# The down projection's weight is read once, in rows of 1 KB, and held in two slots to the middle of the kernel

## Chip, cores and metric

The kernel runs on one core of one Trainium2 chip. The metric is device microseconds for one execution. Before the change the median of three runs is 1683.2 us (1682.9 to 1683.74).

## The reference, cut to what matters

One decode step of a transformer block (4 batch rows, model width D = 512, 32 heads of width 128, a cache of 4096 keys per head, a gated feed-forward of width F = 1792) and its gradients:

```python
q = (layernorm(x) @ wq)                      # 4 x 32 heads
p = softmax(q . k_cache * Dh**-0.5)          # over 4096 keys
h = x + (p . v_cache) @ wo
hh = silu(layernorm(h) @ w1) * (layernorm(h) @ w3)
h2 = h + hh @ w2                             # first output
# then the vector-Jacobian product with grad_out: gradients of x, k_cache, v_cache, wq, wo, w1, w3, w2
```

The caches hold 128 (batch, head) pairs of 1 MB each for K and for V. K is read once and V twice, and two gradients of the size of the caches are written, so nearly all of the 707 MB that the kernel moves are cache. The weight w2 of the change is 1792 x 512 in bf16, 1.8 MB. Two things need it: the gradient of hh, which is grad_out @ w2 transposed, and the block's own output h2.

## The kernel before, in words

**Slots.** One arena in SBUF is cut into 23 slots (`NSLOT`), each large enough for one head of K or V (1 MB over 128 partitions). The list `free` holds the free ones, the one freed longest ago first. `Slot(name)` takes one (L120 on), `give` puts it back. All of this is decided when the program is built, and so are the order of the instructions on each engine and the waits; a DMA into a slot waits until whatever used the slot last has ended. All loads of caches and weights and all large stores are issued by SyncE (SP), in the order in which the code makes them.

**Forward, 64 groups of two heads** (the loop over `gi`). In group gi, with a = 2 gi, the engines do this in the order of the code:

- PE makes the scores of heads a and a+1 from their transposed keys (`S_head`, L392) and gives back the two slots of transposed keys.
- PE and VectorE (DVE) transpose the keys of the next two heads, na = a+2 and nb = a+3, into new slots: `T_pe` (PE, L360, copied out by ScalarE, ACT, L361) and `T_dve` (DVE, L366). A head's keys must have landed for that.
- The softmax of the group goes over DVE, PE and ACT in turn: row maximum (L399, L404, L409, L416), exponential (L424), sum and reciprocal (L430, L435).
- `PK_mul` (DVE, L459) multiplies keys by probabilities, first for head a-1, later in the group for head a; after it the head's K slot is given back and `more_K` loads further heads (L181) while fewer than 8 are held and **more than one slot is free**.
- `M_mm` (PE, L474) multiplies V with that product for heads a-3 and a-2; `M_end` (L484, L488) copies the result into one of eight slots that collect such results (a new one every 16 heads, `Ms`), and gives back the slots of V and of the product; `load_V` (L189) then loads a further V. Three V are held.

The two K loads of a group are thus issued one after `M_end` of head a-3 and `PK_mul` of head a-1, the other after `M_end` of head a-2. The more slots are held by other things, the fewer heads of K are under way.

**w2, first reading.** From group 2 on a generator of side units, `d_hh_units`, is stepped once a group. It loads w2 into two slots (`load_w2`, L543, a row p of the tile holds the 14 weight rows 14 p to 14 p + 13, 7 KB in a row for each slot), transposes it (PE L565, ACT copy L566 into two more slots, where the columns are spread with a stride of 14), gives the two slots of w2 back after some ten groups, and multiplies with grad_out into `d_hhT`.

**End of the forward pass and middle.** From group 61 on free slots go to the last V heads, then to wo (four pages, L591, in rows of 1 KB), w1 and w3 (L585, rows of 3.5 KB). After the last group `attn_page` (PE L522) makes attention times wo in four pages, the layer norm of h follows, and the gate and up projections (PE L918). At the start of this middle part V is loaded for the second time into every slot that is free (`load_V2`, L871: seven heads here, two more after w1 and w3 are done). `w13T` (PE L606, copies by ACT L255 and DVE L257) transposes w1 and w3 in place, in units of up to eight blocks; DVE computes the activations, the last of them `hhT_bf` (L944). Then PE forms `dn_ps` (L952), the gradient that goes back through w1 and w3; from it come the gradient of h, the replicated rows and the first stores of V's gradient (`grad_V`, DVE L844, store L855).

**Backward.** From there on the kernel streams: V's second half in pairs of heads (L1335), the two gradients made by DVE (L844, L1438) and stored (L855, L1310, L1448). A second generator, `side_work`, makes the small outputs in between, stepped twice a head from head 35 on: the gradient of x and wq, then **w2, second reading** (L1143), the transposed rows of hh, a second transposition of hh in the order of w2's rows (L1166 on), the output matmuls (L1174), the DVE add with h (L1180) and the store of the first output (L1182, issued by GpSimd, POOL); then the gradients of w2, w1, w3 and wo.

Of the kernel before, what the change touches and what calls it, by code (L numbers as in the profile page):

```python
# [9 lines left out]
FP32 = mybir.dt.float32  # L10
BF16 = mybir.dt.bfloat16
ALU = mybir.AluOpType
# [16 lines left out]
def kernel(  # L29
# [22 lines left out]
    nc = tc.nc  # L52
    P = nc.NUM_PARTITIONS

    B = A_x.shape[0]
    D = A_x.shape[-1]
# [10 lines left out]
    FC = F // P  # L67
# [7 lines left out]
    x2 = A_x.rearrange("b s d -> (b s) d")  # L75
    g2 = grad_out.rearrange("b s d -> (b s) d")
    o0_2 = out_0.rearrange("b s d -> (b s) d")
# [24 lines left out]
    pers = ctx.enter_context(tc.tile_pool(name="pers", bufs=1))  # L102
# [7 lines left out]
    free = deque(range(NSLOT))  # L110
# [51 lines left out]
            gave(self.i, self.i + 1)  # L162


    rows_t = pers.tile([32 + B, D], FP32, name="rows_t")
    xr, xhat = rows_t[0:B, :], rows_t[32:32 + B, :]
    nc.gpsimd.dma_start(out=xr, in_=x2)
    gr_s = Slot("gr")
# [33 lines left out]
    ident_b = const.tile([P, P], BF16, name="ident_b")  # L202
# [14 lines left out]
    def ones_window(col):  # L217
# [11 lines left out]
                          in_=rowg[:, None, :, None].to_broadcast([P, 4, 8, 4]))  # L229
# [12 lines left out]
    hrows = xr  # L242
# [55 lines left out]
    with ExitStack() as c0:  # L298
# [12 lines left out]
        for h in range(H):  # L311
            for cc in range(DC):
                nc.tensor.matmul(qT_ps[:, h, :], lhsT=wq_s[cc].b(HD)[:, h * Dh:(h + 1) * Dh], rhs=xhatT[:, cc, :],
                                 start=(cc == 0), stop=(cc == DC - 1))
# [4 lines left out]
        for r in range(2):  # L319
            for t_ in range(2):  # L320
                for q in range(4):
                    nc.tensor.matmul(qr_ps[32 * q:32 * (q + 1), 2 * r + t_, :], lhsT=ident_b[:, 64 * r + t_:64 * (r + 1):2],
                                     rhs=qT_bf[:], start=True, stop=True, tile_position=(0, 32 * q))
# [210 lines left out]
    def w13_view(sl, cc):  # L534
        return sl[cc // 2].b(2 * F).rearrange("p (c f) -> p c f", c=2)[:, cc % 2, :]

    def w2_view(sl, fc):
        return sl[fc // 7].b(7 * D).rearrange("p (c j) -> p c j", c=7)[:, fc % 7, :]

    def load_w2():  # L540
        sl = two_slots("w2")
        for i in range(2):
            nc.sync.dma_start(out=sl[i].b(7 * D).rearrange("p (c j) -> p c j", c=7),  # L543
                              in_=B_w2.rearrange("(p c) j -> p c j", c=FC)[:, i * 7:(i + 1) * 7, :])
        return sl


    def d_hh_units():
        w2 = load_w2()
        w2T = two_slots("w2T")  # L550
        gT = fw.tile([P, DC, B], BF16, name="gT", tag="gT", bufs=1)
        yield
        yield
        pt = psX.tile([P, DC, B], FP32, tag="x", name="pt_gT")
        for c in range(DC):
            nc.tensor.transpose(pt[:, c, :], gr[0:B, c * P:(c + 1) * P], ident_f[0:B, 0:B])
        nc.vector.tensor_copy(out=gT[:], in_=pt[:])
        nc.vector.tensor_copy(out=grT[:], in_=pt[:])
        gr_s.give()
        yield  # L560
        for jj in range(DC):
            for i in range(2):
                pt = psT.tile([P, GW, P], BF16, tag="tps", name="pt_w2")
                for k in range(7):
                    nc.tensor.transpose(pt[:, k, :], w2_view(w2, 7 * i + k)[:, jj * P:(jj + 1) * P], ident_b[:])  # L565
                nc.scalar.copy(out=w13_view(w2T, jj).rearrange("q (p c) -> q p c", c=FC)[:, :, i * 7:(i + 1) * 7],  # L566
                               in_=pt[:, 0:7, :].rearrange("q c p -> q p c"))
                yield
        for sl in w2:
            sl.give()  # L570
        ps = psX.tile([P, FC, B], FP32, tag="x", name="dhh_ps")
        for fc in range(FC):
            for jj in range(DC):
                nc.tensor.matmul(ps[:, fc, :], lhsT=w13_view(w2T, jj)[:, fc * P:(fc + 1) * P], rhs=gT[:, jj, :],
                                 start=(jj == 0), stop=(jj == DC - 1))
        nc.vector.tensor_copy(out=d_hhT[:], in_=ps[:])
        for sl in w2T:
            sl.give()


    mid_w = {nm: [] for nm in ("w1", "w3", "wo")}
# [14 lines left out]
    def w13T(n, eng=None):  # L596
        for k in range(n):
            w13T_unit(*tunits.popleft(), eng[k % len(eng)])
# [25 lines left out]
    tunits = deque((nm, i, k) for nm in ("w1", "w3") for i in range(2) for k in range(0, FC, 4))  # L624
# [136 lines left out]
    hhT_bf = pers2.tile([P, FC, B], BF16, name="hhT_bf")  # L761
# [105 lines left out]
    def load_V2(eng=nc.sync):  # L867
        s = nv["next"]
        if s < SP:
            V2s[s] = Slot("V2", vring if vring else free)  # L870
            eng.dma_start(out=V2s[s].heads(), in_=cache_head(A_v_cache, s))  # L871
            nv["next"] += 1

    with ExitStack() as cm:
        mid = cm.enter_context(tc.tile_pool(name="mid", bufs=1, reuse_waits="tile"))
        psA = cm.enter_context(tc.tile_pool(name="psA", bufs=2, space=bass.MemoryType.PSUM))
        psC = cm.enter_context(tc.tile_pool(name="psC", bufs=1, space=bass.MemoryType.PSUM))
# [4 lines left out]
        pt = psA.tile([P, DC, B], FP32, tag="rT", name="pt_hT")  # L882
# [32 lines left out]
        for wi, wt in enumerate((w1, w3)):  # L915
            for fc in range(FC):
                for cc in range(DC):
                    nc.tensor.matmul(gu_ps[:, wi, fc, :], lhsT=w13_view(wt, cc)[:, fc * P:(fc + 1) * P], rhs=hhatT[:, cc, :],  # L918
                                     start=(cc == 0), stop=(cc == DC - 1))
            if wi == 0:  # L920
# [13 lines left out]
                                in1=of4[:, :, None].to_broadcast([NH, B, Dh]), op=ALU.mult)  # L934
# [7 lines left out]
        nc.vector.scalar_tensor_tensor(out=t1[:], in0=t1[:], scalar=1.0, in1=sigT[:], op0=ALU.add, op1=ALU.mult)  # L942
        nc.vector.tensor_tensor(out=d_gateT_bf[:], in0=t2[:], in1=t1[:], op=ALU.mult)
        nc.vector.tensor_tensor(out=hhT_bf[:], in0=siluT[:], in1=gu_ps[:, 1], op=ALU.mult)  # L944
        w13T(len(tunits), "sssvsvsvsvvs")

        dn_ps = psC.tile([P, DC, B], FP32, tag="dn", name="dn_ps")
        for jj in range(DC):
            i_mm = 0
            for (lt, wt) in ((d_gateT_bf, w1), (d_upT_bf, w3)):  # L950
                for fc in range(FC):
                    nc.tensor.matmul(dn_ps[:, jj, :], lhsT=w13_view(wt, jj)[:, fc * P:(fc + 1) * P], rhs=lt[:, fc, :],  # L952
                                     start=(i_mm == 0), stop=(i_mm == 2 * FC - 1))
                    i_mm += 1
        for sl in w1 + w3:
            sl.give()
        rs = Slot("reps")
        kept = [i for i in range(0, NSLOT - 1, 2) if rs.i not in (i, i + 1)][:NPAIR]
        part["pairs"] = {j for i in kept for j in (i, i + 1)}
# [14 lines left out]
        nc.gpsimd.memset(rs.t[:, 3136:ZO + 512], 0.0)  # L974
        for i in range(2):
            nc.gpsimd.memset(halves[64 * i:64 * (i + 1), i:i + 1], 1.0)

        z = mid.tile([P, 2, DC, B], FP32, name="z")
        nc.vector.tensor_copy(out=z[:, 0], in_=dn_ps[:])
# [3 lines left out]
                         start=True, stop=True)  # L983
# [5 lines left out]
                                       in1=hhatT_f[:], op0=ALU.mult, op1=ALU.mult)  # L989
        nc.vector.tensor_tensor(out=u[:], in0=u[:], in1=z[:, 0], op=ALU.add)  # L990
        nc.vector.scalar_tensor_tensor(out=u[:], in0=m[:, 0, None, :].to_broadcast([P, DC, B]), scalar=-1.0 / D,
                                       in1=u[:], op0=ALU.mult, op1=ALU.add)
# [5 lines left out]
        for b0, b1 in ((0, 1), (1, B)):  # L998
            ps = psA.tile([P, B, Dh], FP32, tag="rT", name="rep_ps")
            for b in range(b0, b1):  # L1000
                for jj in range(DC):
                    nc.tensor.matmul(ps[:, b, :], lhsT=dhT[:, jj, b:b + 1].to_broadcast([P, P]), rhs=wo_page(0)[:, 0, jj, :],
                                     start=(jj == 0), stop=(jj == DC - 1))
# [11 lines left out]
    with ExitStack() as c2:  # L1015
# [54 lines left out]
        def side_work():  # L1070
# [60 lines left out]
            for cc in range(DC):  # L1131
# [8 lines left out]
                    flat.give()  # L1140
                    fs.give()
                st.give()
            w2 = load_w2()  # L1143
            yield

            r1, r2 = Slot("rows1"), Slot("rows2")
# [15 lines left out]
            nc.tensor.transpose(pt[:], OT_bf[:], ident_b[:])  # L1162
            yield
            nc.scalar.copy(out=O_sb, in_=pt[:])
            hhT_p = r2.t[:, 3072:3072 + FC * B].rearrange("p (c b) -> p c b", b=B)
            pt = psg.tile([P, FC, B], BF16, tag="gps", name="pt_hhp")  # L1166
            for fc in range(FC):
                nc.tensor.transpose(pt[:, fc, :], hh_rows.rearrange("b (p c) -> b c p", c=FC)[:, fc, :], ident_b[0:B, 0:B])
            yield
            nc.scalar.copy(out=hhT_p, in_=pt[:])  # L1170
            yield
            o2_ps = psx.tile([P, 512], FP32, tag="x2", name="o2_ps")
            for fc in range(FC):
                nc.tensor.matmul(o2_ps[0:B, :], lhsT=hhT_p[:, fc, :], rhs=w2_view(w2, fc), start=(fc == 0), stop=(fc == FC - 1))  # L1174
            for sl in w2:
                sl.give()
            yield
            yield
            h2_bf = rs.t[0:B, 3328:3328 + D]
            nc.vector.tensor_tensor(out=h2_bf, in0=hrows, in1=o2_ps[0:B, :], op=ALU.add)  # L1180
            yield
            nc.gpsimd.dma_start(out=o0_2, in_=h2_bf)  # L1182
            for i in range(2):
                st = Slot("gw2")
                hw = hh_rows[:, i * 7 * P:(i + 1) * 7 * P].rearrange("b (p k) -> b k p", k=7)
# [396 lines left out]
```

## Time and profile before

| | |
|---|---|
| median of the runs | 1683.2 us |
| the profiled execution's own time | 1683.93 us |
| its span, first to last instruction | 1682.1 us |
| PE, DVE, ACT, POOL busy | 75%, 71%, 58%, 22% |
| bytes moved, mean rate | 707.15 MB, 420 GB/s |
| HBM read, written | 422.59 MB, 282.34 MB |
| chain that ended last, by engine | DMA 70%, DVE 11%, PE 11%, issue 3%, ACT 2% |
| loads of K and V of 1 MB, issue to landing, median | 15.7 and 16.1 us |
| w2's four loads of 896 KB, issue to landing | 16.3 to 31.6 us, median 24.8 |

How to read it: the page divides the span into 40 slices of 42 us, with each engine's busy share in tenths and the rate of the DMA engines. The forward pass takes the first 16 or so, the middle the 17th, the backward streaming the rest. In a stretch of busy engines a share near 1.00 in the column of the DMA says that transfers, not instructions, are the limit there. "L181" is line 181 of the kernel. "x16" is a count of instructions merged into one row; what stands in brackets after a row is the idle time just before it, and who ended it. The chain that ended last goes back from the last instruction, at each step to what released it.

### The profile page before, as it was taken

To read this page: it belongs to the slowest core of one execution; us is meant where nothing else is said; L and a number is where in the kernel's file an instruction comes from. 1 tells how busy PE (TensorE), PEld (TensorE's weight loads), DVE (VectorE), ACT (ScalarE), POOL (GpSimd) and SP (SyncE) were. 2 spreads that over 40 slices of the span, in tenths; PEclk is the share of its full clock that TensorE was granted. 3 is DMA by queue.
4 is the path that set the end of the run, shared out by engine and by line. 5 is a ranking of instruction groups with operands and counts; after the bars stand their busy time and mean duration, and the time that the engine had idled before them with its cause. 6 is when DMAs were issued, how large, how long until landed. Compare 5 with 4: busy or idle time off the path is not lost.

```text
span 1682.1 us, 33261 instructions
## 1 busy us (share of the span) xinstructions
PE 1260.9 (75%) x13913; PEld 892.5 (53%) x13913; DVE 1196.4 (71%) x999; ACT 967.7 (58%) x1546; POOL 369.5 (22%) x664
## 2 busy tenths in 40 slices
PE   5999888889889889877777656567666676776750
PEld 4777777777777776634433334444444443444430
DVE  5888888888888887668773667576655656655683
ACT  3565554555445554677666556666665675676650
POOL 1221223222222223112211523211110112111110
PEclk8999999999999999899999878886667766676685
DMA  9999999999999999999999999999999999999996
GB/s 400 425 424 424 425 424 425 425 424 424 419 424 400 425 424 395 407 406 426 426 426 427 429 430 430 430 430 429 431 430 429 430 430 430 430 429 430 431 430 282
DMA packets 80981, 707.15 MB, mean 420 GB/s; under 512 B 8748, under 2 KB 12984, under 8 KB 15296
## 3 DMA queue, kind: packets, MB, share of 16 engines
q1 hardware_dynamic: 80416, 704.94, 99.4%
q8 instruction: 109, 1.79, 0.4%
q14 instruction: 40, 0.33, 0.0%
q0 software_dynamic: 416, 0.10, 0.0%
HBM read 422.59 MB, written 282.34 MB: 419 GB/s over the span
## 4 chain that ended last, share of the span: by engine, by line
DMA 70%; DVE 11%; PE 11%; issue 3%; ACT 2%; DVEq 0%; SPq 0%; POOL 0%; ACTq 0%; POOLq 0%
DMA out_dram<-arena 43%; DMA arena<-in_A_v_cache_dram 25%; DVE arena L1438 8%; PE M_ps L474 4%; DMA arena<-in_A_k_cache_dram 2%; DVE arena L844 1%; DVE arena L459 1%; PE pt_tps L360 1%; PE kP_ps L484 1%; PE S_ps L392 1%; PE pt_P L445 1%; PE b_ps L416 1%; ACT Pn L438 1%; ACT E L424 1%; PE pt_w L606 1%
## 5 line engine op out<-in xcount | busy, mean ns | idle before, releaser
L810 ACT COPY arena<-pt_tps 128x1024 bf16<-128x1024 bf16 x512 | 491.0, 1026 | 244.6 <-PE pt_tps L809 242.7
L809 PE MATMUL pt_tps<-ident_f,arena 128*128 128x128 f32 x2048 | 398.5, 347 | 200.9 <-DMA arena<-in_A_v_cache_dram 116.3
L809 PEld LDWEIGHTS pt_tps<-ident_f,arena 128*128 128x128 f32 x2048 | 291.6, 176 | 369.2 <-issue 193.4
L1438 DVE TENSOR_TENSOR arena<-arena 128x8192 bf16<-128x8192 bf16 x48 | 212.4, 4425 | 217.6 <-DMA out_dram<-arena 199.6
L474 PE MATMUL M_ps<-arena 128*128 128x130 bf16 x4096 | 285.4, 222 | 47.6 <-DMA arena<-in_A_v_cache_dram 45.9
L459 DVE TENSOR_TENSOR arena<-arena 128x4096 bf16<-128x4096 bf16 x128 | 290.9, 2273 | 14.9 <-POOL arena L455 14.2
L474 PEld LDWEIGHTS <-arena 128*128 128x128 bf16 x4096 | 250.5, 99 | 70.2 <-DMA arena<-in_A_v_cache_dram 63.1
L1438 DVE TENSOR_TENSOR arena<-dS,arena 128x8192 bf16<-128x8192 bf16 x48 | 212.3, 4425 | 63.6 <-DMA out_dram<-arena 63.6
L366 DVE STREAM_TRANSPOSE arena<-arena 128x512 f32<-128x512 f32 (+1 forms) x258 | 239.9, 947 | 0.0
L361 ACT COPY arena<-pt_tps 128x1024 bf16<-128x1024 bf16 x128 | 123.5, 1015 | 197.9 <-PE pt_tps L360 174.8
L1435 POOL COPY arena<-arena 128x128 bf16<-128x128 bf16 x48 | 48.2, 1005 | 397.6 <-DVE arena L1438 266.6
L372 POOL TENSOR_TENSOR W<-qrep,wmask 128x128 bf16<-128x128 bf16 x128 | 110.4, 862 | 83.1 <-PE S_ps L392 68.5
L455 POOL COPY arena<-P_all 128x64 bf16<-128x64 bf16 x128 | 32.1, 251 | 405.4 <-ACT P_all L449 385.0
L1347 POOL COPY arena<-arena 64x4 bf16<-64x4 bf16 x96 | 80.5, 838 | 120.5 <-PE dP_ps L1367 112.1
L438 ACT ACTIVATE Pn<-E,rl 128x1024 bf16<-128x1024 f32 x64 | 73.6, 1149 | 36.2 <-DVE rl L435 35.9
L1367 PE MATMUL dP_ps<-arena 128*32 128x512 bf16 x768 | 86.7, 492 | 6.0 <-ACT arena L810 5.9
L449 ACT COPY P_all<-pt_P 32x64 bf16<-32x64 bf16 x256 | 51.9, 203 | 61.5 <-PE pt_P L445 59.3
L844 DVE TENSOR_TENSOR arena<-dS,arena 128x4096 bf16<-128x4096 bf16 x32 | 73.8, 2310 | 14.7 <-DMA out_dram<-arena 13.7
L392 PE MATMUL S_ps<-arena,W 128*32 128x256 bf16 x1536 | 79.6, 284 | 0.9 <-DVE arena L366 0.8
L484 PE MATMUL kP_ps<-arena,onesw 128*32 128x512 bf16 x1024 | 80.2, 390 | 0.0
L844 DVE TENSOR_TENSOR arena<-P,arena 128x4096 bf16<-128x4096 bf16 x28 | 63.8, 2287 | 18.9 <-DMA out_dram<-arena 18.9
L1034 PE MATMUL gps<-arena 4*128 4x512 bf16 x110 | 45.4, 441 | 39.7 <-ACT arena L1028 39.7
(258 smaller groups left out, 1390.0 us busy)
## 6 DMA issues: line engine op xcount, KB each, us to landing
out_dram<-arena SPq DMA_DIRECT2D x96, 2048.0 KB, 27.5
arena<-in_A_v_cache_dram SPq DMA_DIRECT2D x160, 1024.0 KB, 16.1
arena<-in_A_k_cache_dram SPq DMA_DIRECT2D x128, 1024.0 KB, 15.7
arena<-in_A_v_cache_dram SPq DMA_DIRECT2D x48, 2048.0 KB, 31.7
out_dram<-arena SPq DMA_DIRECT2D x72, 1024.0 KB, 19.8
arena<-in_A_wq_dram SPq DMA_DIRECT2D x8, 1024.0 KB, 17.8
arena<-in_B_w_dram SPq DMA_DIRECT2D x8, 896.0 KB, 14.4
out_dram<-arena SPq DMA_DIRECT2D x6, 896.0 KB, 26.2
```

The lines of the kernel that those rows point to most:

```text
L361: nc.scalar.copy(out=KT[:, c * GW:(c + 1) * GW, :], in_=pt[:])
L366: nc.vector.transpose(out=KT[:, c * w_:(c + n) * w_], in_=Kn[:, c * w_:(c + n) * w_])
L372: nc.gpsimd.tensor_tensor(out=W[:, hl], in0=qrep[:, :, s:s + 1].to_broadcast([P, 4, 32]), in1=wmask[:, hl, None, :].to_broadcast([P, 4, 32 ...
L392: nc.tensor.matmul(st["S"][32 * c:32 * (c + 1), :], lhsT=lhsT, rhs=rhs, start=(hl == 0 and k == 0), stop=(hl == G - 1 and k == 3), tile_po ...
L438: nc.scalar.activation(out=st["Pn"][:], in_=st["E"][:, :, None, :].to_broadcast([P, JQ, 4, 32]), func=AF.Copy, scale=rl[:])
L459: nc.vector.tensor_tensor(out=PK[:, :, 0:Dh].rearrange("p j (r t) -> p j r t", t=2), in0=Ks[s].heads().rearrange("p j (r t) -> p j r t", t=2),
L474: nc.tensor.matmul(hold["M"][:], lhsT=Vn[:, j, :], rhs=PK[:, j, :], start=(j == 0), stop=(j == SJ - 1))
L484: nc.tensor.matmul(hold["kP"][32 * q:32 * (q + 1), :, :], lhsT=ones_window(w), rhs=PK[:, j0:j0 + 4, 0:Dh], start=(w == 0 and c == 0), stop ...
L809: nc.tensor.transpose(ptw[:, jj, :], w[:, 4 * g + jj, :], ident_f[:])
L810: nc.scalar.copy(out=v.rearrange("p (j d) -> p j d", d=Dh)[:, g * GW:(g + 1) * GW, :], in_=pt[:])
L844: nc.vector.tensor_tensor(out=dst.rearrange("p j (r t) -> p j r t", t=2), in0=col2[:, :, None, :].to_broadcast([P, SJ, Dh // 2, 2]), in1=r ...
L1438: nc.vector.tensor_tensor(out=dst.rearrange("p (j r t) -> p j r t", r=Dh // 2, t=2), in0=col2[:, :, None, :].to_broadcast([P, 2 * SJ, Dh / ...
```

## The change

The weight is loaded once, in its natural blocks: row p of a tile holds the weight rows p, p+128, and so on, which makes rows of 1 KB in HBM. The evacuation of the transposed weight becomes contiguous. The two slots are not given back after the transposition but kept in `mid_w["w2"]`. In the middle, after five of the remaining twelve units of `w13T`, PE makes the block's output from `hhT_bf` and the held weight, 14 matmuls into two column groups; then the two slots are given back and V loads take them. DVE adds the two partial sums to h in a third block of `rows_t` after dn's matmuls have been put in the list, POOL copies the sum to bf16 and stores it. The second reading, the second transposition of hh and the output matmuls in `side_work` go.

```diff
-    rows_t = pers.tile([32 + B, D], FP32, name="rows_t")
+    rows_t = pers.tile([64 + B, D], FP32, name="rows_t")
...
-                              in_=B_w2.rearrange("(p c) j -> p c j", c=FC)[:, i * 7:(i + 1) * 7, :])
+                              in_=B_w2.rearrange("(c p) j -> p c j", p=P)[:, i * 7:(i + 1) * 7, :])
...
-        w2 = load_w2()
+        w2 = mid_w["w2"] = load_w2()
...
-                nc.scalar.copy(out=w13_view(w2T, jj).rearrange("q (p c) -> q p c", c=FC)[:, :, i * 7:(i + 1) * 7],
-                               in_=pt[:, 0:7, :].rearrange("q c p -> q p c"))
+                nc.scalar.copy(out=w13_view(w2T, jj)[:, i * 7 * P:(i + 1) * 7 * P].rearrange("q (c p) -> q c p", p=P),
+                               in_=pt[:, 0:7, :])
                 yield
-        for sl in w2:
-            sl.give()
...
-        w13T(len(tunits), "sssvsvsvsvvs")
+        w13T(5, "sssvsvsvsvvs"[:5])
+        o2_ps = psC.tile([P, D], FP32, tag="cols", name="o2_ps")
+        for fc in range(FC):
+            c = fc % 2
+            nc.tensor.matmul(o2_ps[32 * c:32 * c + B, :], lhsT=hhT_bf[:, fc, :], rhs=w2_view(mid_w["w2"], fc),
+                             start=(fc < 2), stop=(fc >= FC - 2), tile_position=(0, 32 * c))
+        for sl in mid_w["w2"]:
+            sl.give()
+        while len(free) > 0:
+            load_V2()
+        w13T(len(tunits), "sssvsvsvsvvs"[5:])
...
+        h2 = rows_t[64:64 + B, :]
+        nc.vector.tensor_tensor(out=h2, in0=hrows, in1=o2_ps[0:B, :], op=ALU.add)
+        nc.vector.tensor_tensor(out=h2, in0=h2, in1=o2_ps[32:32 + B, :], op=ALU.add)
         rs = Slot("reps")
...
+        h2_bf = rs.b()[64:64 + B, 512:512 + D]
+        nc.gpsimd.tensor_copy(out=h2_bf, in_=h2)
+        nc.gpsimd.dma_start(out=o0_2, in_=h2_bf)
...
-            w2 = load_w2()
             yield
...
-            pt = psg.tile([P, FC, B], BF16, tag="gps", name="pt_hhp")
-            for fc in range(FC):
-                nc.tensor.transpose(pt[:, fc, :], hh_rows.rearrange("b (p c) -> b c p", c=FC)[:, fc, :], ident_b[0:B, 0:B])
...
-            o2_ps = psx.tile([P, 512], FP32, tag="x2", name="o2_ps")
-            for fc in range(FC):
-                nc.tensor.matmul(o2_ps[0:B, :], lhsT=hhT_p[:, fc, :], rhs=w2_view(w2, fc), start=(fc == 0), stop=(fc == FC - 1))
-            for sl in w2:
-                sl.give()
...
-            nc.vector.tensor_tensor(out=h2_bf, in0=hrows, in1=o2_ps[0:B, :], op=ALU.add)
-            yield
-            nc.gpsimd.dma_start(out=o0_2, in_=h2_bf)
```

More of the change, by code (lines that the diff above doesn't have):

```diff
@@ L1164, in side_work @@
             nc.scalar.copy(out=O_sb, in_=pt[:])
-            hhT_p = r2.t[:, 3072:3072 + FC * B].rearrange("p (c b) -> p c b", b=B)
-            pt = psg.tile([P, FC, B], BF16, tag="gps", name="pt_hhp")
-            for fc in range(FC):
-                nc.tensor.transpose(pt[:, fc, :], hh_rows.rearrange("b (p c) -> b c p", c=FC)[:, fc, :], ident_b[0:B, 0:B])
             yield
-            nc.scalar.copy(out=hhT_p, in_=pt[:])
-            yield
-            o2_ps = psx.tile([P, 512], FP32, tag="x2", name="o2_ps")
-            for fc in range(FC):
-                nc.tensor.matmul(o2_ps[0:B, :], lhsT=hhT_p[:, fc, :], rhs=w2_view(w2, fc), start=(fc == 0), stop=(fc == FC - 1))
-            for sl in w2:
-                sl.give()
-            yield
-            yield
-            h2_bf = rs.t[0:B, 3328:3328 + D]
-            nc.vector.tensor_tensor(out=h2_bf, in0=hrows, in1=o2_ps[0:B, :], op=ALU.add)
-            yield
-            nc.gpsimd.dma_start(out=o0_2, in_=h2_bf)
             for i in range(2):
```

## The prediction

> **What bounds the kernel now.** I read the page's slices first, then stretches, then the DMA issues, and last the chain that ended last, around the middle.
>
> ```profile
> DMA  9999999999999999999999999999999999999996
> GB/s 400 425 424 424 425 424 425 425 424 424 419 424 400 425 424 395 407 406 426 426 426 427 429 430 430 430 430 429 431 430 429 430 430 430 430 429 430 431 430 282
> ...
> q1 hardware_dynamic: 80416, 704.94, 99.4%
> ```
>
> The DMA engines are busy in every slice, at 424 GB/s in the forward pass and 430 in the backward. Two things can move the time: bytes, and stretches in which the engines have nothing queued. The low slices (12 and 15 to 17, counted from 0) are the places where that nearly happens; 15 to 17 are the end of the forward pass and the middle:
>
> ```profile
> 600.00:630.00 30.00, 27.05 (x454) 22.48 (x452) 26.70 (x28) 15.50 (x38) 9.22 (x20) 1.00 1.01 424
> 630.00:660.00 30.00, 26.96 (x440) 21.30 (x438) 23.51 (x25) 15.48 (x41) 7.21 (x15) 1.00 0.99 407
> 660.00:690.00 30.00, 28.24 (x429) 23.43 (x427) 15.73 (x35) 14.52 (x23) 10.83 (x39) 0.83 1.02 401
> 690.00:720.00 30.00, 22.98 (x279) 16.42 (x276) 24.29 (x27) 20.33 (x26) 5.07 (x12) 0.94 0.97 385
> ```
>
> The columns are PE, PEld, DVE, ACT and POOL busy, granted clock, DMA share and GB/s. What feeds the engines is the number of K loads under way, and that is a matter of free slots. Counting the program's takes and gives of its 23 slots (they are fixed when it is built), before holds 8 K heads at the start of a group up to group 57 and 7 in groups 58 to 61. A K load takes 17.1 us from issue to landing between 20 and 400 us, 14.3 us between 500 and 601 and 12.1 us between 604 and 631 (medians): each slot lost is a megabyte less in the queue. In groups 58 to 61 SP issues (first start us, then duration):
>
> ```profile
> 616.97 0.33 SPq L181 DMA_DIRECT2D arena<-in_A_k_cache_dram  x1
> 621.12 0.33 SPq L189 DMA_DIRECT2D arena<-in_A_v_cache_dram  x1
> 621.54 0.38 SPq L181 DMA_DIRECT2D arena<-in_A_k_cache_dram  x1
> 623.02 0.51 SPq L189 DMA_DIRECT2D arena<-in_A_v_cache_dram  x1
> 626.05 0.33 SPq L181 DMA_DIRECT2D arena<-in_A_k_cache_dram  x1
> 630.20 0.33 SPq L189 DMA_DIRECT2D arena<-in_A_v_cache_dram  x1
> 630.63 0.37 SPq L181 DMA_DIRECT2D arena<-in_A_k_cache_dram  x1
> ```
>
> Two K loads per group, the second right behind a V load. PE transposes the next two heads (L360, x16 for both):
>
> ```profile
> 614.84 1.05 PE L360 MATMUL pt_tps<-ident_b,arena 128*128 128x128 bf16 x16
> 623.83 1.05 PE L360 MATMUL pt_tps<-ident_b,arena 128*128 128x128 bf16 x16
> 632.90 0.61 PE L360 MATMUL pt_tps<-ident_b,arena 128*128 128x128 bf16 x8
> 633.84 0.62 PE L360 MATMUL pt_tps<-ident_b,arena 128*128 128x128 bf16 x8 [0.33 <-DMA arena<-in_A_k_cache_dram]
> ```
>
> Already with 7 heads the second transpose of a group (call it B) waits for its K, 0.33 us here and 0.75 us in group 62. And the chain that ended last says what follows:
>
> ```profile
> 630.63 13.05 DMA arena<-in_A_k_cache_dram
> 643.68 0.05 issue
> 643.73 0.62 PE pt_tps L360 x8
> ```
>
> That is the last K head, 127. From 643.73 to 716.43 us the chain holds only PE, ACT, DVE and issue, no transfer. So the landing of the last K sets the start of the backward stores, and a delay of it is carried to the end.
>
> **The change, part by part.**
>
> *Second reading gone.* 1.835 MB less (2 x 896 KB) in the backward half, where 430 GB/s move without a gap: 1.835 / 0.430 = **-4.3 us**. Its 14 matmuls, 14 small transposes and DVE add leave a side list whose engines are 55 to 75% busy there: 0.
>
> *First reading in rows of 1 KB* instead of 7 KB. The nearest row is wo, also in 1 KB rows: its four pages land 2.7, 2.7 and 2.8 us apart, the 3.5 KB rows of w1 and w3 2.2 us per 896 KB, K and V 2.45 us per MB. Extra: 1.75 x 0.27 = **+0.5 us** (0 to 1). The Trainium skill, "DMA: Bandwidth & Descriptors", section Specifications, gives 512 B as the smallest transfer at line rate; by it this term is 0 and the sum 0.5 lower; wo's landings speak against it.
>
> *Evacuation of the transposed weight* (L566, ACT, x8, 1.13 us each, 82 to 151 us) becomes contiguous: ACT is half idle there, 0 either way.
>
> *Two slots held from group 2 to the middle.* By the same count after has 8 K heads until group 41, 7 to group 49, 6 in most of 50 to 57, and 5 in groups 58 to 62. With 7 and 6 the queue only gets shorter: at 6, B's K is issued at the group's first K issue (616.97 for a B at 624.4, 7.4 us) and a lone 1 MB load needs less, see below. With 5, the heads held are the one awaiting its product, the two in use and the two to be transposed now: the K of B is the *second* issue of the group just before. That is 630.63 for a B at 633.5, 2.9 us; B to the next such issue is compute, 624.4 to 630.63, **6.2 us** (row maximum, exponential, product L459, then the slot that M_end gives). The loop is 6.2 us plus a landing, and to hold the DMA's own pace of 9.85 us per group (four loads) the landing may take 3.6 us. What the trace has of nearly empty queues:
>
> ```profile
> DMA to landing us min/median/max: 4.9/8.2/11.2
> ...
> DMA to landing us min/median/max: 6.4/7.5/8.7
> ```
>
> The upper line is wq (L174), the first four loads of the kernel, issued 0.4 us apart: the first lands after 4.9, the second after 7.3 us. The lower is a pair of V loads in the middle (L871). Ours is second of a pair: I take 7.3, bounds 4.9 (as if no V stood before it) and 8.7. From before's issue at 611.67 us (group 58) B comes at 619.0, then every 13.5 us: 632.5, 646.0, 659.5. Before has the last at 643.7. **+15.8 us**; with 4.9, 616.6 + 3 x 11.1 = 649.9, +6.2; with 8.7, 620.4 + 3 x 14.9 = 665.1, +21.4. The same page of the Trainium skill, section "Anatomy of one DMA — SWDGE (gpsimd) path", fits 2.0 us + bytes/436e3 for another issuing path, an estimate of 6.4 us for the second of a pair 0.4 us apart; by it the loop is 12.6 us, the term +12.1 and the sum 3.7 lower. The trace's first load, 4.9 against the fit's 4.4, stands a little above it.
>
> *Middle.* The 14 output matmuls stand in PE's list between the fifth and sixth transpose unit of w1/w3, behind hhT_bf (L944, ends 685.83), when PE would start unit six at 685.8. PE is nearly without gaps from there to the dn matmuls at 689.67, which start the way to the first store. attn_page's matmuls of the same shape cost 1.03 us per 8 when they alternate between two column groups, 1.89 when not: 1.8 to 3.4 us; the clock here is 0.68, against 1.00 there: **+2.4 us**. Behind it wait seven transpose units, their ACT and DVE copies, dn. The two DVE adds (0.69 each, by L528) fit the 2.2 us in which DVE waits for dn; without that cover +1.4. POOL's copy (0.6 by L1150) and output DMA stand before only dhT_f, used much later. Two of the first seven V loads now wait for these matmuls; the queue, 14 to 20 us from issue to landing there, runs out for 1 to 3 us, but the stores wait for the chain, not for it: no further term.
>
> Sum against the profiled 1683.93 us (span 1682.1): 15.8 + 2.4 + 0.5 - 4.3 = +14.4, 1698.3. The median shown is 0.7 below the profiled time: **1697.6**.
>
> **Rivals.** A difference under about 0.2% (3.4 us) can't be told from none.
> 1. *No starving, or it is given back* (not slower). Place: B in groups 59 to 62. If K landed within 3.6 us the loop would keep pace, or if the way from the last K to the first store had DMA waits that shrink with the shorter queue, the delay would be absorbed. Price: the 15.8 goes, 1681.8. For it: landing times fall with every slot less. Against: no 1 MB load in the trace landed under 4.9 us, and the chain has no DMA piece from 643.73 to 716.43. 12%.
> 2. *As 1, and the output matmuls hide* in PE's waits for copies: 1679.4, faster. 5%.
> 3. *Starving begins with 6 heads.* If a lone K then takes 8.7, its loop is 8.7 + 1.7 = 10.4 us against 9.85 for eight groups, +4, with the long landing at 5 heads too: 1683.2 + 21.4 + 4 + 2.4 + 0.5 - 4.3 = 1707. 5%.
> The loads and issues built have two DMAs fewer on SP, so the reading is really gone.
>
> **Numbers.** Forecast 78%: 1697.6, own range by the bounds 1686 (6.2 + 1.8 - 4.3) to 1705 (21.4 + 3.4 + 1 - 4.3). Rivals 1 and 2 stay below, 3 above. Faster 5%, same 12%, slower 83%.
>
> **What would show it.** Group periods (S_head to S_head) near 13 us between 605 and 660 us, with PE's L360 waiting some 4 us each on in_A_k_cache, DMA share there near 0.75, GB/s near 320; K landings about 7 us. The dn matmuls 18 us later than before; the bytes 705.3 MB; the backward half at 430 GB/s, 4.3 us shorter. Wrong: those L360 waits under 1 us each, or a way from the last K to the first store shorter than 73 us.

## The result and the profile after

The changed kernel takes 1712.6 us (median of 5 runs, 1711.66 to 1714.7) against 1683.34 us (5 runs, 1682.9 to 1684.34) before: ratio 1.0176, 95% interval 1.0164 to 1.0187. It is slower by 29.3 us; 1697.6 was forecast, within 1686 to 1705. The sign and the place were right, the size was off by a factor of two. The profiled execution has a span of 1710.8 us and a time of 1712.6 us.

The rows of the page that answer to those shown of before:

```profile
DMA  9999999999999986999999999999999999999996
...
GB/s 402 420 424 425 425 424 424 426 419 425 406 424 388 403 333 243 399 381 426 426 426 427 429 429 430 430 429 430 429 431 430 429 430 429 430 430 430 429 432 288
...
q1 hardware_dynamic: 81664, 703.10, 98.1%
```

Slices 14 and 15 (599 to 684 us) fall from 424 and 395 GB/s to 333 and 243; no other slice loses more than 25. The bytes are 1.84 MB fewer. The stretches (columns PE, PEld, DVE, ACT, POOL busy, granted clock, DMA share, GB/s):

```profile
600.00:630.00 30.00, 23.03 (x326) 18.33 (x327) 19.08 (x22) 12.33 (x30) 6.82 (x15) 0.88 0.87 343
630.00:660.00 30.00, 20.25 (x261) 17.62 (x262) 15.54 (x16) 8.69 (x20) 5.28 (x11) 0.73 0.73 267
660.00:690.00 30.00, 25.02 (x326) 20.58 (x325) 18.33 (x20) 11.17 (x29) 4.77 (x9) 0.82 0.75 270
690.00:720.00 30.00, 28.85 (x413) 22.38 (x410) 14.57 (x32) 14.57 (x26) 10.79 (x39) 0.83 1.04 411
```

Two columns fall together: the DMA share, as forecast, and the clock of TensorE, which was 1.00 in the first two of these stretches before. SP's issues from the end of group 58 to the end of group 59:

```profile
616.47 0.38 SPq L181 DMA_DIRECT2D arena<-in_A_k_cache_dram  x1
617.96 0.33 SPq L189 DMA_DIRECT2D arena<-in_A_v_cache_dram  x1
627.72 0.33 SPq L181 DMA_DIRECT2D arena<-in_A_k_cache_dram  x1
632.54 0.33 SPq L189 DMA_DIRECT2D arena<-in_A_v_cache_dram  x1
633.99 0.33 SPq L181 DMA_DIRECT2D arena<-in_A_k_cache_dram  x1
```

The K of the second transpose goes out at 616.47 and 633.99, 17.5 us apart (13.5 forecast). In between PE does this (start, duration; x16 or x24 matmuls in one row; in brackets the wait and who ended it):

```profile
624.71 1.03 PE L360 MATMUL pt_tps<-ident_b,arena 128*128 128x128 bf16 x8 [4.67 <-DMA arena<-in_A_k_cache_dram]
625.53 0.42 PE L404 MATMUL x_ps<-ident_f,mx 128*1 128x128 f32 x1
625.75 1.94 PE L474 MATMUL M_ps<-arena 128*128 128x130 bf16 x16
627.62 1.01 PE L416 MATMUL b_ps<-gm,selg 1*128 1x1 f32 x4
628.56 1.04 PE L484 MATMUL kP_ps<-arena,onesw 128*32 128x512 bf16 x8
629.53 0.59 PE L430 MATMUL l_ps<-rs,bsum 128*128 128x1 f32 x2
629.98 2.76 PE L474 MATMUL M_ps<-arena 128*128 128x130 bf16 x24
632.53 0.96 PE L445 MATMUL pt_P<-ident_b,Pn 128*128 128x128 bf16 x8
633.33 0.63 PE L474 MATMUL M_ps<-arena 128*128 128x130 bf16 x8
```

The same rows of group 59 before take 0.62, 0.27, 1.10, 0.60, 0.62, 0.38, 1.57, 0.62 and 0.63 us: all but the last are longer by 1.5 to 1.8 times. Three of them before:

```profile
615.84 1.10 PE L474 MATMUL M_ps<-arena 128*128 128x130 bf16 x16
617.40 0.62 PE L484 MATMUL kP_ps<-arena,onesw 128*32 128x512 bf16 x8
618.56 1.57 PE L474 MATMUL M_ps<-arena 128*128 128x130 bf16 x24
```

The stretches of 3 us of the changed kernel (columns as above) say why:

```profile
619.00:622.00 3.00, 0.62 (x8) 0.45 (x8) 1.31 (x3) 1.01 (x1) 1.24 (x4) 1.00 1.02 421
622.00:625.00 3.00, 0.29 (x3) 0.30 (x4) 0.00 (x0) 0.00 (x0) 0.00 (x0) 0.67 1.01 426
625.00:628.00 3.00, 3.00 (x26) 2.74 (x25) 1.92 (x3) 1.01 (x1) 0.24 (x1) 0.50 0.09 38
628.00:631.00 3.00, 3.00 (x23) 2.15 (x24) 0.84 (x2) 1.46 (x5) 0.00 (x0) 0.50 0.75 246
631.00:634.00 3.00, 3.00 (x37) 2.89 (x38) 2.67 (x2) 1.02 (x4) 0.00 (x0) 0.63 0.51 145
634.00:637.00 3.00, 2.96 (x64) 2.33 (x58) 2.29 (x2) 0.63 (x3) 1.63 (x2) 1.00 0.90 322
```

First all engines stand still for a transfer (622 to 625, DMA at 426 GB/s), then the DMA engines stand still for TensorE (625 to 628, 38 GB/s), and TensorE works at a clock of 0.50. The two wait for each other in turn. The chain that ended last carries the loop through its pieces:

```profile
616.47 8.19 DMA arena<-in_A_k_cache_dram
624.71 1.03 PE pt_tps L360 x8
...
633.99 8.44 DMA arena<-in_A_k_cache_dram
642.47 1.04 PE pt_tps L360 x8
...
651.42 7.14 DMA arena<-in_A_k_cache_dram
658.61 1.03 PE pt_tps L360 x8
...
668.00 6.30 DMA arena<-in_A_k_cache_dram
674.34 1.04 PE pt_tps L360 x8
```

From group to group (row maximum to row maximum) groups 59 to 62 take 17.6, 17.4, 16.6 and 14.0 us, 65.6 together (619.27 to 684.89); before 9.9, 9.1, 9.5 and 9.9, 38.3 together (614.48 to 652.79): +27.3. Group 51 takes 14.8 instead of 9.1. The last row maximum starts at 684.9 instead of 652.8 us, +32.1.

The middle, with the output matmuls:

```profile
707.99 1.61 PE L916 MATMUL gu_ps<-hhatT,arena 128*128 128x4 bf16 x56 [0.77 <-ACT warm L889]
...
718.26 1.81 PE L947 MATMUL o_ps<-arena,hhT_bf 128*4 128x512 bf16 x14
...
722.70 0.49 PE L960 MATMUL dn_ps<-d_gateT_bf,arena 128*128 128x4 bf16 x14
```

From the gate projections to dn it is 14.71 us; before, 676.00 to 689.67, 13.67. The output matmuls cost +1.0. So dn starts +33.0 later, and the span ends +28.7 later: 4.3 us come back behind dn.

### The profile page after: what moved, and what is told of

It reads as the page before. It is cut to its first block, busy times and chain, and to the rows that moved or that the text cites. A ratio compares the mean times of both kernels' runs of the same rounds, so it can differ in the third digit from the quotient of the medians.

```text
span 1710.8 us, 33205 instructions
## 1 busy us (share of the span) xinstructions
PE 1284.1 (75%) x13899; PEld 907.6 (53%) x13899; DVE 1195.9 (70%) x1000; ACT 967.3 (57%) x1545; POOL 371.3 (22%) x665
## 4 chain that ended last, share of the span: by engine, by line
DMA 67%; PE 15%; DVE 10%; issue 3%; ACT 2%; POOL 1%; DVEq 0%; SPq 0%; ACTq 0%; POOLq 0%
DMA out_dram<-arena 37%; DMA arena<-in_A_v_cache_dram 22%; DMA arena<-in_A_k_cache_dram 8%; DVE arena L1434 7%; PE M_ps L474 6%; PE pt_tps L360 2%; PE kP_ps L484 1%; DVE arena L842 1%; PE b_ps L416 1%; PE S_ps L392 1%; PE pt_P L445 1%; ACT Pn L438 1%; POOL P L824 1%; DMA arena<-in_A_wq_dram 1%; PE pt_w L604 1%
## 5 line engine op out<-in xcount | busy, mean ns | idle before, releaser
L474 PE MATMUL M_ps<-arena 128*128 128x130 bf16 x4096 | 296.1, 227 | 31.1 <-DMA arena<-in_A_v_cache_dram 29.3
L474 PEld LDWEIGHTS <-arena 128*128 128x128 bf16 x4096 | 262.8, 102 | 52.3 <-DMA arena<-in_A_v_cache_dram 43.0
L1431 POOL COPY arena<-arena 128x128 bf16<-128x128 bf16 x48 | 56.9, 1186 | 409.5 <-DVE arena L1434 279.3
L1343 POOL COPY arena<-arena 64x4 bf16<-64x4 bf16 x96 | 72.2, 752 | 130.6 <-PE dP_ps L1363 123.1
L360 PE MATMUL pt_tps<-ident_b,arena 128*128 128x128 bf16 x1024 | 74.5, 226 | 31.5 <-DMA arena<-in_A_k_cache_dram 31.5
L360 PEld LDWEIGHTS <-arena 128*128 128x128 bf16 x1024 | 63.2, 101 | 35.7 <-DMA arena<-in_A_k_cache_dram 34.6
## 6 DMA issues: line engine op xcount, KB each, us to landing
out_dram<-arena SPq DMA_DIRECT2D x96, 2048.0 KB, 27.3
arena<-in_A_k_cache_dram SPq DMA_DIRECT2D x128, 1024.0 KB, 14.1
```

The costliest lines, as they stand in the source:

```text
L360: nc.tensor.transpose(pt[:, i, :], Kn[:, c * GW + i, :], ident_b[:])
L474: nc.tensor.matmul(hold["M"][:], lhsT=Vn[:, j, :], rhs=PK[:, j, :], start=(j == 0), stop=(j == SJ - 1))
```

## Experiments

Theory: with 5 heads of K held, the K of the second transpose (B) can be asked for only at the end of a way on PE and DVE that begins when the previous B's K has landed; landing and way add up, and the wait in between costs TensorE its clock, which makes the way longer. Rivals: the shorter queue itself (fewer bytes under way, so a lower rate whatever the order); the middle or the rows of 1 KB; a cost per slot rather than a threshold.

| label | kernel | median us (runs) | ratio to before, 95% |
|---|---|---|---|
| e1_hold_only | before, w2's slots held | 1714.47 (1713.62 to 1716.9) | 1.0171 to 1.0198 |
| e2_read_once_free | read once, not held | 1679.34 (1678.6 to 1680.35) | 0.9962 to 0.9984 |
| e3_pe_busy | after, 48 idle matmuls ahead of B | 1708.25 (1701.72 to 1709.77) | 1.0121 to 1.0154 |
| e4_k_first | after, K ahead of V | 1697.49 (1696.09 to 1699.39) | 1.0068 to 1.0096 |
| e5_last_slot | after, K may take the last slot | 1692.9 (1691.7 to 1698.0) | 1.0047 to 1.0075 |
| e6_hold_one | before, one slot held | 1688.28 (1685.26 to 1691.03) | 1.0014 to 1.0035 |
| e7_before_last_slot | before, rule of e5 | 1684.34 (1682.61 to 1684.73) | 0.9991 to 1.0009 |
| e8_late_b | after, B later | 1687.99 (1686.11 to 1690.43) | 1.0017 to 1.0035 |
| e9_late_both | after, both transposes later | 1690.92 (1688.43 to 1692.0) | 1.0030 to 1.0055 |
| e10_late_b_last_slot | e8, last K load of a group from 58 on may take the last slot | 1685.91 (1685.16 to 1691.2) | 1.0008 to 1.0026 |
| e11_pe_busy_76 | e3 with 76 matmuls | 1702.45 (1699.01 to 1707.51) | 1.0101 to 1.0133 |
| e12_before_late_b | before, B later | 1689.07 (1687.41 to 1689.34) | 1.0019 to 1.0041 |

### Which part of the change costs: e1, e2

```diff
-        w2 = load_w2()
+        w2 = mid_w["w2"] = load_w2()
...
-        for sl in w2:
-            sl.give()
...
-        w13T(len(tunits), "sssvsvsvsvvs")
+        w13T(5, "sssvsvsvsvvs"[:5])
+        for sl in mid_w["w2"]:
+            sl.give()
+        while len(free) > 0:
+            load_V2()
+        w13T(len(tunits), "sssvsvsvsvvs"[5:])
```

> The kernel before, with one part of the change alone: the two slots of w2 are kept from the transposition to the same place in the middle and given back there; the second reading and the output matmuls stay where they were. Theory (the held slots cost the time: with 5 heads of K the second K load of a group comes too late for the transposition of the next group, and the DMA queue runs empty): the whole loss and none of the saving, 1712.6 + 4.3 - 1 = about 1716 us, group periods of 16 to 18 us in groups 59 to 62 and a granted TensorE clock of about 0.5 in half of that time. Rival (the loss comes from the output matmuls, the later V loads or the other row order): within 3 us of before, 1681 to 1687 us.

Holding alone costs 30.7 us (1714.47 against 1683.74 of the same chip); groups 59 to 62 take 17.2, 17.4, 13.6 and 16.7 us, with 7 KB rows and no output matmuls in the middle. The whole loss, and a little more, is the two slots.

e2 is the changed kernel with the two slots given back after the transposition and no output matmuls: its first output is h alone.

```diff
-        w2 = mid_w["w2"] = load_w2()
+        w2 = load_w2()
...
+        for sl in w2:
+            sl.give()
         ps = psX.tile([P, FC, B], FP32, tag="x", name="dhh_ps")
...
-        h2 = rows_t[64:64 + B, :]
-        nc.vector.tensor_tensor(out=h2, in0=hrows, in1=o2_ps[0:B, :], op=ALU.add)
+        nc.vector.tensor_copy(out=h2, in_=hrows)
```

> The changed kernel without the hold: w2 is read once, in rows of 1 KB, its slots are given back after the transposition as before, the output matmuls and the second reading are left out, so that the first output lacks the feed-forward part (it is h alone). Theory: only the saving of the bytes is left, minus what 1 KB rows cost: 1683.3 - 4.3 + 0.5 = 1679.5 us. Rival (the new row order or the dropped side work moves something else): over 1683 us.

One reading less saves 4.4 us (1679.34 against 1683.74). That is the whole prize of the change; 1.835 MB at 430 GB/s are 4.3.

### Threshold or a price per slot: e6

Against e1, one of the two slots is given back after the transposition and only the other is held:

```diff
+        w2[0].give()
...
-        for sl in mid_w["w2"]:
-            sl.give()
+        mid_w["w2"][1].give()
```

> The kernel before, but one of the two slots of the second weight (the second one) is held to the middle and the other given back as before; the second reading and the output in the side work stay. By the count 7 heads of K are held in groups 51 to 57 and 6 in 58 to 61. Theory (a threshold: nothing is lost until the number of heads falls to 5): within 4 us of the kernel before, 1683 to 1688 us. Rival (each slot costs the same): half of what holding both cost (1714.5 against 1683.7), 1699 us.

One slot costs 4.5 us, two cost 30.7. At 1688.28 the run is 0.3 above the upper end that the theory gave and 10.7 below the rival's figure: not a price per slot, though not quite free either. Group 59 takes 14.8 us here, 61 11.2, the other two 9.1 and 10.2: one large stall, which does not repeat at that size.

### Order of the loads: e4

```diff
             M_end(m2)
+            if 58 <= gi <= 61 and len(Ks) + kdone["n"] < NH:
+                load_K(len(Ks) + kdone["n"])
             load_V(m2 + VQ)
```

> The changed kernel, where in groups 58 to 61 the second K load of a group is issued before the V load that stood ahead of it; same loads, same number of heads. Theory (the landing of that K bounds the loop, and 2.4 us of its 8 are the V ahead of it): K lands in 5 to 6 us and is issued some 0.5 to 1.5 us earlier, the wait of PE falls from 5 to about 2 us and the clock does not fall: 4 groups x 3 to 6 us, 1689 to 1701 us. Rival (the loop is bound by V or by the compute chain, not by K): within 3 us of 1712.6.

With the same slots and bytes, and B's K issued with no V ahead of it, 0.4 us (at full clock) to 1.4 us (at half clock) sooner after the B before it, 15.1 us of the 29.3 go. Groups 59 to 62 take 14.2, 10.6, 16.0 and 9.3 us, and those K land 4.7 to 7.0 us after issue. The landing of that one load is in the path; the shorter queue alone does not explain the loss.

### TensorE's clock: e3, e11

```diff
+            if 59 <= gi <= 62:
+                busy = psX.tile([P, 512], FP32, tag="x", name="busy_ps")
+                for _ in range(48):
+                    nc.tensor.matmul(busy[:, 0:P], lhsT=ident_b[:], rhs=ident_b[:], start=True, stop=True)
             T_pe(nb)
```

e11 has 76 in place of 48. The results are not used.

> The changed kernel with 48 idle matmuls (identity by identity, about 4 us at full clock) on PE just before the transposition that waits for K, in groups 59 to 62. Theory (a TensorE that waited 4 to 6 us comes back at half the granted clock and makes the way from that transposition to the next K issue 9.3 us long instead of 6.2): the clock stays near 1.0, the way shrinks to 6.2 to 7, the period from about 17 to 14 us, the time to 1712.6 - 4 x 2.5 = about 1702 us. Rival (the slow rows come from elsewhere, or the extra work delays PE): 1712 us or more.

> The changed kernel with 76 instead of 48 matmuls of the identity ahead of the second transpose of groups 59 to 62, some 4.5 us at full clock, so that TensorE's own idle time there is under 1 us. They compute nothing that is used. Theory (the way from the second transpose to the next K load is 9.3 instead of 6.2 us because TensorE's granted clock falls after an idle wait of 4 to 6 us): the clock of 610 to 660 us stays at 1.00 and all periods of 59 to 62 are 14 to 15 us, landing 8.2 plus 6.3; the time is 1700 to 1704 us, lower than 1708 with 48 matmuls, where the clock fell in the third of these groups in the profiled execution. Rival (those rows are long for another reason, such as the slots' contention): periods 17 us, 1712 us.

More work for TensorE, and the kernel is faster: 4.4 us with 48 matmuls and 10.2 with 76 (medians, against 1712.6). In e3's profiled execution, the fastest of its runs (1701.72), the clock was kept in groups 59 and 60, 14.1 and 14.5 us long, and lost in 61, 16.9; of the other three, 6 to 8 us slower, no trace shows the clock. In e11's it was kept through all four. Stretches of e3, then of e11:

```profile
600.00:630.00 30.00, 26.06 (x438) 21.24 (x438) 22.53 (x23) 13.39 (x34) 7.39 (x16) 1.00 0.90 343
630.00:660.00 30.00, 24.28 (x360) 21.01 (x361) 15.87 (x19) 10.28 (x24) 4.90 (x12) 0.89 0.75 279
```

```profile
630.00:660.00 30.00, 27.93 (x465) 24.05 (x463) 18.70 (x20) 11.70 (x29) 5.64 (x13) 1.00 0.78 287
660.00:690.00 30.00, 28.00 (x455) 22.81 (x453) 19.95 (x19) 12.10 (x31) 5.44 (x12) 1.00 0.89 331
```

In e11 groups 59 to 62 take 13.2, 14.4, 13.2 and 13.8 us, 54.6 together against 65.6: at a full clock the loop is what the prediction had, 13.5 per group, and the clock's fall adds 11.0. The way from B to the next such issue is 6.25 us again (B at 628.90, SP's issue at 635.15; 6.28 and 6.26 in the next two). One part of the expectation failed: the clock fell ahead of these groups (0.69 in 610 to 620 us, group 58 takes 13.7 us), and groups 53 and 55 stalled too, so this execution, at 1707.51, is the slowest of its five.

### One head more: e5, and its control e7

```diff
-        while len(Ks) + kdone["n"] < min(NH, s + 8) and len(free) > 1:
+        while len(Ks) + kdone["n"] < min(NH, s + 8) and len(free) > spare:
...
+        spare = 0 if gi >= 50 and gi != 57 else 1
...
             kP_turn(m1)
+            more_K(a + 1)
```

> The changed kernel, but in groups 50 to 62 (not 57) a K load may take the last free slot too, so that by the program's count 6 or 7 heads of K are held in 50 to 57, 5 in 58 and 6 in 59 to 61. Nothing is left out. Theory (the closed loop of slot, landing and compute exists only with 5 heads; with 6 the K of the second transpose is issued a whole point earlier): periods of the groups 59 to 62 under 12 us, the clock of 600 to 660 us above 0.9, no stall of 5 us in group 51, time 1684 to 1690 us. Rival (the loss comes from the bytes that are missing in the queue whatever the order, so that a megabyte more in the queue gains its share of two): half of the loss of 33 us stays, 1697 us or more.

> The kernel before, with the same rule as the run that lets a K load take the last free slot in groups 50 to 62; nothing is left out. A control: both theories expect no change, 1682 to 1685 us. If it were faster by over 3 us, the rule would be a gain of its own, and what it brings in the changed kernel could not be put down to the loop.

e7 changes nothing, as expected. e5 takes back 19.7 of the 29.3 us, yet 1692.9 is above the 1690 that the theory allowed and below the rival's 1697. Groups 52 to 57 run at 9.1 to 9.7 us, but 51 (15.4), 59 (16.7) and 61 (13.7) still stall. Group 59 is the heir of 58, which has only 5 heads at its start: the two K that group 59 transposes go out at 607.49 and 611.65, its two transposes wait 2.32 and 1.82 us for them, and the clock is 0.50 from 619 to 628. That 6 heads are enough was too simple; why 61 stalls with 6 was not tried by itself.

### Opening the loop: e8, e9, e10, and the control e12

e8 moves B's transpose; e9 moves the first one too, behind the first K load; e10 is e8 in which, from group 58 on, the last K load of a group may take the last free slot; e12 is e8's edit in the kernel before.

```diff
+        late = gi == 51 or 58 <= gi <= 62
...
-            T_pe(nb)
+            if not late:
+                T_pe(nb)
...
             load_V(m2 + VQ)
         weights(gi)
+        if late:
+            T_pe(nb)
...
```

> The changed kernel with the same slots and the same loads, but in groups 51 and 58 to 62 the second transpose of the group (L360 and its share of L366) stands behind the second M_end and the second product, so that a late K no longer stands before the softmax that leads to the next K load. Nothing is left out. Theory (the loss is the loop landing plus way on PE and DVE from B to the next K load): the two run side by side, the period is back at 10 to 11 us, K loads of a group are issued 9 to 10 us apart from those of the next, time 1681 to 1686 us. Rival (the loss is a queue that is too short for the DMA engines, wherever the transpose stands): share and rate in 600 to 660 us stay near 0.75 and 300 GB/s, time 1700 us or more.

> The kernel before, with the second transpose of groups 51 and 58 to 62 behind the second M_end; nothing is left out. A control for the runs that move it in the changed kernel. Both theories expect no gain: 1683 to 1686 us, since with 7 heads the second transpose waits under 1 us. If it were faster by over 3 us, what the move brings in the changed kernel could not be put down to the loop.

> The changed kernel with the same two slots held, but in groups 51 and 58 to 62 both transposes of a group (L360 and L366) stand later: the first behind the first product of the group and the K loads behind that, the second behind the second M_end. Nothing is left out. In the run with only the second transpose moved, the pair of K loads was issued at 621.32, the first transpose ended its wait at 629.47 and the next pair went out at 632.30: landing 8.15 plus a way of 2.83, a period of 10.98 us. Theory (the loop is landing plus whatever way on PE and DVE lies from the waiting transpose to the next K load): now that way is near 0, the loop 8.2 us, shorter than the DMA's 9.85, so the periods of 59 to 62 fall to 9.9 to 10.3 and the time by 2 to 4 us to 1684 to 1686 us. Rival (with so short a queue the DMA engines give 388 GB/s in 600 to 660 us however the loads are issued): no change, 1688 us.

> The changed kernel with the second transpose of groups 51 and 58 to 62 behind the second M_end, and from group 58 on the last K load of a group may take the last free slot: by the count 6 heads of K in 59 to 61 instead of 5. Nothing is left out. Theory (with the loop opened, one head more in the queue lets a K load go out a point earlier, its landing hidden): periods of 59 to 62 under 10.3 us, time 1684 to 1686 us. Rival (the heads held do not matter once the transpose is moved): 1688 us.

e8 holds w2's two slots and starts the same groups with 5 heads, and 24.6 of the 29.3 us are gone: groups 59 to 62 take 10.5 to 11.0 us at a clock of 1.00. The move does two things, though. The transpose no longer stands ahead of the softmax; and as it takes its own slot later, the first K load of a group finds one slot more, so that B's K goes out in a pair with the other (621.32 and 621.74 us), half a group earlier than in the changed kernel, and 6 heads are held from there to the group's end. e8 opens the loop at both places and does not tell them apart, nor does it keep the queue quite as short. Against the shorter queue alone stand e4, which has the heads of the changed kernel and loses half as much, and e11, where work on TensorE alone brings 10.2 us.

What is left of the loss in e8 the control explains, against what I had expected of both. The move is not free: e12, with 7 heads, loses 5.3 us by the move alone, with groups 59 to 62 at 10.5 us each. Its transposes:

```profile
622.84 0.62 PE L360 MATMUL pt_tps<-ident_b,arena 128*128 128x128 bf16 x8
...
626.31 0.61 PE L360 MATMUL pt_tps<-ident_b,arena 128*128 128x128 bf16 x8
...
633.33 0.62 PE L360 MATMUL pt_tps<-ident_b,arena 128*128 128x128 bf16 x8
```

No bracket stands behind these rows: no transpose waits for a K. The moved order is itself 10.5 us long on PE, DVE and ACT (the scores of the next group wait 0.56 us for ACT's copy, the next gap on PE is 0.38 for DVE). In e9 it is 11.3 us in each group, again without a wait of L360 for a transfer, and slower, so its expected gain did not come; no rate of the DMA engines need be the reason. In e10 groups 59 to 62 are at exactly 10.5, the length of the moved order, so nothing of the loop is left there; the periods under 10.3 that I expected did not come. Between e12 and e10, which share the move, the change is worth -3.2 us (1689.07 to 1685.91): that fits the saving of the second reading less the output matmuls and the rows, -4.3 + 1.0 + 0.5 = -2.8, with the loop gone, but the two intervals of the table overlap, and e10 also has its rule for the last slot. None of the complete kernels is faster than the one before.

## Why the prediction was right and wrong

- **Second reading, -4.3**: right. e2 shows -4.4, with the rows of 1 KB in it; in the profile dn starts +33.0 and the span ends +28.7.
- **Rows of 1 KB, +0.5**: right. w2's two loads land 2.34 and 2.47 us behind the load before them, 2.13 and 2.19 in rows of 7 KB: 4.81 - 4.32 = +0.5.
- **The loop, +15.8 (6.2 to 21.4)**: the mechanism was right (the K of B asked for in the group just before, SP's issue behind M_end, L360 waiting 3.4 to 5.5 us, no transfer on the way from the last K to dn); the size was +27.3 and outside the bounds. **The step that failed is "B to the next such issue is compute, 6.2 us"**: in the kernel after it is 624.71 to 633.99, 9.3 us. The 6.2 us were read from rows at a clock of 1.00, and I carried them into groups in which the same PE waits 4.67 us; the clock fell to 0.50. In the list of signs I even wrote that wait down. The Trainium skill, "TensorE: Matmul & The Clock Gate", part 1 on the HAM clock gate, says that the array is set to half its rate after an idle window of about 3.4 us. The trace agrees, with 1.00 before the wait and 0.50 behind it; the rule spoke against this term and the prediction did not weigh it. e11 gives its price: 65.6 - 54.6 = 11.0 us in four groups, 10.2 us by the medians. With the clock kept, the way is 6.25 us and the loop 54.6 / 4 = 13.65 us, against the 6.2 and 13.5 forecast.
- **Landing, 7.3 (4.9 to 8.7)**: the four in the chain are 8.19, 8.44, 7.14 and 6.30, mean 7.5; within the bounds.
- **"With 7 and 6 the queue only gets shorter"**, cost 0: wrong. Group 51 lost 5.7 us, and 4.8 of the 32.1 lie ahead of group 59. In group 49 a further collecting slot is taken, 5 heads are left at the start of group 50, and both K that group 51 transposes are asked for only within group 50 (from 527.40 on, for a transpose that then starts at 537.06). The two transposes wait 1.07 and 2.02 us, and the clock is 0.50 from 538 to 544 behind them. I counted the heads per stretch, not the group in which the count changes.
- **Output matmuls, +2.4 (1.8 to 3.4)**: too high, +1.0. They took the 1.8 us of two column groups (x14 at 1.81), but PE had had a gap of 0.68 us in the gate projections, and that is gone.
- **Evacuation, DVE adds, POOL's copy, 0**: nothing in the chain speaks against it; they were not tried alone.
- **Rivals**: 1 and 2 (not starving) fell at once. 3 (long landings, starving with 6 heads, 1707) was nearer in size, but for another reason.
- **The range**: its lower end, 6.2 + 1.8 - 4.3 on 1683.2, adds up to 1686.9, not 1686; nothing hangs on it.
- **Signs listed**: L360's waits, share 0.73 to 0.75, landings (median 7.1) and bytes came as written. Periods of "near 13 us" were 14.0 to 17.6, the rate of 320 was 267 to 343, dn came 33 us later and not 18.

In sum, in the profiled executions: +27.3 in four groups, +4.8 ahead of them (the rows' 0.5 among it), +0.9 up to dn, -4.3 behind it: +28.7. Of the 14.3 us between this and the forecast of +14.4, 11.5 are in the loop, nearly all of it the clock by e11's 11.0, and 4.3 in group 51 and its like, less 1.5 in the middle.

## What to carry to other kernels

Where a slot is taken from a stream, count how many loads ahead are left at its tightest group, and in the group in which the count changes: as long as the load for a step is asked for one step earlier than its wait, the lost depth was cheap (4.5 us for one slot here), and where landing and way came to stand in one loop it cost all at once (30.7 us for two). Price such a loop with the rows as they will run, not as they ran: waits of 3.4 to 5.5 us per turn halved the clock of TensorE behind them here. Moving the waiting instruction behind the ones that lead to the next load opened the loop without any more memory (it also took its slot later, which let the load go out earlier), but a move in a tuned order has its own price, so run it as a control in the kernel before.

## What the runs showed of the hardware

- How long the half clock lasts differs. Behind the first three waits of the changed kernel's loop it lasted about 8 to 9 us of work: B starts at 624.71, 642.47 and 658.61, and the rows are back at full speed from about 633.3, 650.3 and 667.4 on, though in the table of 3 us PE is busy throughout 625 to 631 at 0.50. Behind the fourth (3.40 us, B at 674.34) they are back by 677.95, 3.6 us later, and in e4 behind a wait of 3.77 us (B at 623.69) by 626.58, 2.9 us later. The same part of that page of the Trainium skill has the full clock come back after about 3.4 us of sustained work: the trace agrees for these last two waits and not for the first three. What decides between them no run here shows.
- The clock also fell behind shorter waits: 1.07 and 2.02 us, one soon after the other, in group 51 (0.50 from 538 to 544), and 2.32 and 1.82 us in group 59 of e5. The fall does not need a single wait of the 3.4 us that the page gives; the measurement decides.
- Idle matmuls that keep TensorE busy through a wait made the kernel 10 us faster than letting it wait (e11).
- A DMA share near 1.00 does not by itself say that transfers are the limit; the note on reading the page, ahead of the prediction, puts that too strongly. In e9 this stretch stands at 0.97 with 388 GB/s, while L360 waited for no transfer and the groups were 11.3 us long by compute:

```profile
610.00:650.00 40.00, 33.68 (x520) 25.14 (x513) 30.37 (x25) 19.86 (x47) 8.12 (x19) 1.00 0.97 388
```

- Why the landing of a K behind a V takes 6.3 to 8.4 us and that of a lone one 4.7 to 4.9, though a megabyte takes 2.45 us in the steady stream, stays open.
